# Gated mix of two spectral filters: third row block in two transfers, an eviction moved behind it, two evictions of stage 4 on VectorE, row sums one group sooner

## The chip, the core and the metric

The kernel runs on one core of a Trainium2 chip. That core has five engines that are used here: TensorE (PE; its weight loads are listed apart as PEld), VectorE (DVE), ScalarE (ACT), GpSimd (POOL) and SyncE (SP, which issues most of the DMAs). Each engine works through its own list of instructions in order, and the lists wait for each other through semaphores. The metric is the device time of one execution in microseconds (us); lower is better. The time before is the median of three runs.

## The reference

The input x has 2048 rows of 1024 numbers in bf16. Two branches, A and B, each take a two-dimensional real Fourier transform of x, multiply it with a complex weight of 2048 x 513, and transform back. A gate per row, the sigmoid of the row's product with a vector, mixes the two.

```python
g = sigmoid((x * gate_w).sum(-1, keepdims=True))
def branch(x, w_r, w_i):
    X = rfft2(x.astype(float32)) * (w_r + 1j * w_i)
    return irfft2(X, s=(2048, 1024)).astype(bfloat16)
out = g * branch(x, A_w_r, A_w_i) + (1 - g) * branch(x, B_w_r, B_w_i)
```

## The kernel before

All transforms are matrix products with constant matrices. A list of operations is written down in program order with what each reads and writes (`P.add`); from it each engine gets its own instructions in that same order, with a semaphore wait wherever another engine's result is needed. So the order in the Python text is the order on every engine: an instruction whose wait is not over holds up everything behind it on its engine. A weight or x tile is waited for by the whole transfer that carries it.

The work goes through these stages.

- **Stage 1** (`fold`, `stage1`). The rows come in four blocks, c = 0 to 3, each of 1 MB on 128 partitions; `XPARTS` says in how many transfers, and blocks 2 and 3 lie where weights are loaded later. VectorE folds a block (L348: sums for h = 0, differences for h = 1, each with s = 0, 1). TensorE then makes 32 matmuls a block (L387), in four units (h, j) of eight; each unit fills two of the eight PSUM banks, and is copied to `FT` by ScalarE (L398) or, for three units of blocks 1 to 3, by VectorE (L396). A unit's banks come free for the next block when that copy is done.
- **Weights** (`wload`). 44 transfers on SP's queue, in six lots with a semaphore each. The lots follow x and the constants on the same queue. Lot 2 holds what products 2 to 4 need, lot 3 products 5 and 6, lot 4 product 7, lot 5 (the last) product 8.
- **Stages 2 and 4** (`step(i)`, i = 0 to 15). In each step TensorE does stage 4 of i (L482, two PSUM banks; bank 3 is shared by neighbouring steps, so the second half of stage 4 of i+1 waits for the copy of i), then stage 2 of i+2 (L456, L465), then a few small matmuls for the gate (L514). ScalarE copies both results (L486 for stage 4 into one of six `X` slots, L471 for stage 2). `swap(i)` exchanges real and imaginary rows of the copy by two DMAs, on POOL's queue for i up to 8 and on SP's behind the weights after that.
- **Products** (`product`, L501, VectorE): `ORDER[i]` lists which products come behind step i; the second number of an entry is 0 for the copy itself and 1 for the swapped one. They write the weights' own tiles.
- **Stage 5** (`group`): 32 groups of 16 matmuls (L610) and one copy each (L621 on ScalarE, L619 on VectorE), over four PSUM slots in turn. The first group follows step 14; groups 1 to 7 need the first-half products, of which (8, 0) and (8, 1) with h0 = 0 are the last. The row sums for the gate are finished on VectorE (`row_sums`), spread by 32 matmuls (`zsum`, L557), go through a sigmoid on ScalarE (L560), and become masks (`gate_mask`, L566, VectorE). `rbgen` (L597, VectorE, 16 of them) multiplies the masks into the matrices of stage 6.
- **Stages 6 and 7** for 16 row groups r (L751 copied by L766; L781 with an even part copied by L788). For most r, VectorE makes two sums of PSUM and copy (L828) and POOL adds and subtracts these (L833, 22 in all); for r = 5, 9, 12, 14, 15 VectorE does it alone (L814, L792). Each r ends in a store of 256 KB. Row group 13 is the last that POOL works on.

After the first stage 6 pieces the remaining `rbgen` follow: some at once, then one behind each of the next r. The lines at the end of stage 5 that set the order before are:

```python
group(spare(), g, "dve" if n in (2, 3) else "act")
if n == 2: zsum([spare(), spare()])
if n in (3, 5): gate_mask(n // 2 - 1)
for _ in range((3 < n < 14) + (n == 6)): rbgen(rb.pop(0), "dve")
```

Of the kernel before, what the change touches and what calls it, by code (L numbers as in the profile page):

```python
# [5 lines left out]
ACT = mybir.ActivationFunctionType  # L6
# [228 lines left out]
def bass_gated_mix__spectral_gfnet__spectral_gfnet__prompt_kernel(nc, A_x, A_w_r, A_w_i, B_x, B_w_r, B_w_i, gate_w, out):  # L235
# [36 lines left out]
    def bank(b):  # L272
        return ("ps", b)
# [9 lines left out]
    P = Prog()  # L283
# [12 lines left out]
    def xloc(c):  # L296
        return WT[c // 2], ((c % 2) * 32 + 24) * RWS[c // 2]

    XPARTS = {0: ((0, 1), (1, 1), (2, 2)), 1: ((0, 2), (2, 2)), 2: ((0, 4),), 3: ((0, 2), (2, 2))}
    XALL = [("x", c, q0) for c in range(4) for q0, n in XPARTS[c]]  # L300
    P.add("pool", lambda e: e.memset(sl(CL, GRo, [(1, 256)]), 0.0), w=["GRz"])
    P.add("pool", lambda e: e.memset(DUM[:], 0.0), w=["DUM"])
    for _ in range(18):
        P.add("pe", lambda e: e.matmul(ps(7 * 512, [(1, 256)]), sl(CL, GRo, [(1, 128)]), sl(CL, GRo, [(1, 256)]), start=True, stop=True),
              r=["GRz"], w=[bank(7)])
# [34 lines left out]
    def fold(c, q0, n, h):  # L340
        t, o = xloc(c)
        o += q0 * 1024
        fo = (c % 2) * 4096 + q0 * 1024
        for s in range(2):
            g = 1 - 2 * s
            i0 = sl(t, o + 511 * s, [(1024, n), (256 * g, 2), (g, 128)])
            i1 = sl(t, o + (512 if s else 1023), [(1024, n), (-256 * g, 2), (-g, 128)])
            P.add("dve", lambda e, s=s, i0=i0, i1=i1: e.tensor_tensor(  # L348
                out=sl(XF, fo + h * 512 + s * 256, [(1024, n), (384 - 512 * s, 2), (1, 128)]), in0=i0, in1=i1, op=ALU.subtract if h else ALU.add),
                r=[("x", c, max(a for a, _ in XPARTS[c] if a <= q0))], w=[("xf", c % 2, q, h, s) for q in range(q0, q0 + n)])  # L350

    def folds(c):
        parts = XPARTS[c]
# [17 lines left out]
    def stage1(c):  # L371
        nonlocal cnt
        us = [(cnt + k) % 4 for k in range(4)]
        cnt += 4
        parts = XPARTS[c] if c == 0 else ((0, 4),)
        for q0, n in parts:
            for h in range(2):
                for j in range(2):
                    u = us[2 * h + j]
                    for q in range(q0, q0 + n):  # L380
                        r = 4 * c + q
                        base = (c % 2) * 4096 + q * 1024 + h * 512
                        o = ps(u * 1024 + q * 256, [(1, 256)])
                        for s in range(2):
                            lh = sl(XF, base + 256 * s + 128 * j, [(1, 128)])
                            rh = sl(MM, r * 128, [(2048 * s, 2), (1, 128)])
                            P.add("pe", lambda e, o=o, lh=lh, rh=rh, s=s: e.matmul(o, lh, rh, start=(s == 0), stop=(s == 1)),  # L387
                                  r=[("xf", c % 2, q, h, s ^ j), ("M", c), ("NM", c)], w=[bank(2 * u + q // 2)])
                    if q0 + n < 4:
                        continue  # L390
                    for m0, mn in ((0, 32), (32, 96)) if (c, h, j) == (3, 1, 1) else ((0, 128),):
                        src = ps(u * 1024 + m0, [(128, 2), (1, mn), (256, 4)])
                        dst = sl(FT, h * 8192 + j * 2048 + 16 * m0 + 4 * c, [(4096, 2), (16, mn), (1, 4)])
                        kw = dict(r=[bank(2 * u), bank(2 * u + 1)], a=[("F1", h, j)] + [("F1a", h, j)] * (m0 == 0))
                        if (c, h, j) in ((1, 0, 1), (2, 1, 1), (3, 0, 1)):
                            P.add("dve", lambda e, s=src, d=dst: e.tensor_copy(d, s), **kw)  # L396
                        else:
                            P.add("act", lambda e, s=src, d=dst: e.activation(d, s, ACT.Copy), **kw)  # L398
# [21 lines left out]
    last1 = [P.ops["pe"][-1]]  # L420
    SEQ = [(0, 0), (0, 1), (0, 2), (1, 0)] + [(0, p) for p in range(3, 8)] + [(1, p) for p in range(1, 8)]
    CSo = lambda i: (i % 3) * 1024
    Xk = lambda i: (i + 1) % NX
# [50 lines left out]
    def stage4(i):  # L474
# [8 lines left out]
                                                                                      start=(m == 0), stop=(m == 1)),  # L483
                          r=[("CS", i % 3), "CK"], w=[bank(bk[pm])])
        dst, src = sl(XF, Xo(i), [(1, 1024)]), ps(bk[0] * 512, [(256, 2), (512, 2), (1, 256)])
        P.add("act", lambda e: e.activation(dst, src, ACT.Copy), r=[bank(k) for k in bk], w=[("X", Xk(i))], after=last1)  # L486

    def swap(i):
        eng = ("pool", "sp")[i > 8]
# [133 lines left out]
    def group(u, g, eng):  # L623
        group_mm(u, g, range(8), lambda q: q)
        group_out(u, g, eng, 0, 8, 1, 0, [("Z", 0), ("Z", 1)])
# [27 lines left out]
    def step(i):  # L653
# [5 lines left out]
        if i == 15:  # L659
            dma("sp", "U5", sl(FT, U5o, [(2048, 8), (1, 1024)]).bitcast(u16), cst["U5"].ap().rearrange("p (a b) -> p a b", a=8), w=["U5"], after=[last2])  # L660


    ORDER = (((0, 0),), ((1, 0),), ((2, 0),), ((3, 0),), ((0, 1), (4, 0)), ((1, 1), (2, 1)), ((3, 1),), ((5, 0, 0, 2, 2), (4, 1), (5, 1, 0, 2, 2)),
             ((7, 0), (7, 1)), ((8, 0, 0, 1), (8, 1, 0, 1), (8, 0, 1, 1)), ((8, 1, 1, 1), (9, 0, 0, 2, 2)), ((9, 1, 0, 2, 2),), ((11, 0, 0, 2, 2),),
             ((11, 1, 0, 2, 2),))

    def products(i):
# [22 lines left out]
    def spare():  # L690
        slots.append(slots.pop(0))
        return slots[-1]
# [27 lines left out]
    for n, g in enumerate(range(16, 32)):  # L720
        if n == 14:
            last_groups([spare(), spare()])
        elif n < 14:
            group(spare(), g, "dve" if n in (2, 3) else "act")
        if n == 2:
            zsum([spare(), spare()])
        if n in (3, 5):
            gate_mask(n // 2 - 1)
        for _ in range((3 < n < 14) + (n == 6)):
            rbgen(rb.pop(0), "dve")  # L730
    assert slots[-2:] == [1, 2]
    last5 = P.ops["pe"][-1]

# [114 lines left out]
    stage6_mm(1, range(2, 4), (0,))  # L848
    stage6_mm(1, range(4), (1,))
    stage6(1, False)  # L850
    for _ in range(2):
        rbgen(rb.pop(0), "dve")
    for r in range(16):
        for q in {0: (), 1: (2,), 2: (3, 4)}.get(r, (r + 2,) if r < 14 else ()):
# [69 lines left out]
```

## Time and profile before

| what | value |
|---|---|
| median of three runs | 123.36 us (123.10 to 123.36) |
| the profiled execution's own time | 123.46 us |
| its span, first to last instruction | 121.4 us |
| busy: PE, DVE, ACT, POOL | 114.2, 101.0, 99.5, 40.9 us |
| DMA | 26.11 MB, mean 215 GB/s |
| granted TensorE clock | 1.00 throughout |
| stage 1 on PE | 5.5 to 21.5 us |
| stages 2 and 4 on PE | 21.5 to 50.7 us |
| stage 5 on PE | 50.7 to 84.7 us |
| stages 6 and 7, to the last store | 84.7 to 121.4 us |

Times inside the span are counted from its first instruction. The profiled execution took 2.06 us more than its span; what lies around the span is the same for both kernels as far as the profile tells. The span is read stage by stage, since no single engine is the limit of all four.

### The profile page before, as it was taken

The numbers are of one execution on the slowest core, as the hardware profiler recorded it, in microseconds if no ns is written. First come the engines' busy times: TensorE is split into PE (matmuls) and PEld (weight loads), VectorE is DVE, ScalarE is ACT, GpSimd is POOL, SyncE is SP. The second block draws the span as 40 slices with busy tenths as digits, with TensorE's granted clock in tenths as the row PEclk, the third lists the DMA queues.
The fourth block names the chain that finished last, engine by engine and source line by source line (L and its number), as shares of the span: only waits on it lengthen the run. The fifth ranks groups of instructions, "written<-read, shape, count | busy, mean of one in ns | idle before, by whom it ended". The sixth has DMA issues, their size and how long they took to land.

```text
span 121.4 us, 3690 instructions
## 1 busy us (share of the span) xinstructions
PE 114.2 (94%) x1556; PEld 95.3 (78%) x1556; DVE 101.0 (83%) x160; ACT 99.5 (82%) x119; POOL 40.9 (34%) x47
## 2 busy tenths in 40 slices
PE   6898999999999999999999999999999999999950
PEld 4566688887766766689999999999899969898630
DVE  0378999989798699999999848998689997787890
ACT  4249985999999999999999988999779858867610
POOL 1000042016655600000000000000039999999990
PEclk9999999999999999999999999999999999999999
DMA  3999999999999999840699400000001222424556
GB/s 89 298 406 432 403 326 359 354 348 352 363 361 368 363 363 373 301 173 23 174 397 388 174 0 5 0 5 0 0 5 56 100 102 93 173 86 150 204 200 231
DMA packets 17536, 26.11 MB, mean 215 GB/s; under 512 B 2096, under 2 KB 11056, under 8 KB 17392
## 3 DMA queue, kind: packets, MB, share of 16 engines
q1 hardware_dynamic: 16224, 23.00, 54.0%
q0 software_dynamic: 864, 2.36, 5.4%
q10 hardware_dynamic: 432, 0.52, 1.4%
q8 instruction: 12, 0.20, 0.7%
q14 instruction: 4, 0.03, 0.1%
HBM read 17.48 MB, written 4.19 MB: 178 GB/s over the span
## 4 chain that ended last, share of the span: by engine, by line
PE 71%; POOL 9%; DMA 6%; DVE 3%; issue 3%; SPq 2%; ACT 2%; POOLq 1%; DVEq 0%
PE PS L610 26%; PE PS L482 12%; POOL WA L833 9%; PE PS L751 7%; PE PS L387 7%; PE PS L781 6%; PE PS L456 6%; DMA WB<-in_A_x_dram 6%; PE PS L465 3%; PE PS L514 2%; DVE XF L348 2%; SPq L290 2%; POOLq L863 1%; ACT XF L486 1%; PE PS L557 1%
## 5 line engine op out<-in xcount | busy, mean ns | idle before, releaser
L833 POOL TENSOR_TENSOR WA<-WA 128x512 bf16<-128x512 f32 x22 | 28.5, 1326 | 47.6 <-DVE WA L828 47.6
L610 PE MATMUL PS<-CL,WB 128*128 128x128 bf16 x256 | 31.7, 226 | 0.0
L610 PE MATMUL PS<-CL,WA 128*128 128x128 bf16 x256 | 31.6, 223 | 0.0
L610 PEld LDWEIGHTS PS<-CL,WB 128*128 128x128 bf16 x256 | 31.3, 145 | 0.2
L610 PEld LDWEIGHTS PS<-CL,WA 128*128 128x128 bf16 x256 | 31.3, 145 | 0.1
L621 ACT ACTIVATE WB<-PS 128x1024 bf16<-128x1024 f32 (+1 forms) x30 | 28.4, 1020 | 0.6 <-PE PS L610 0.5
L501 DVE TENSOR_TENSOR WB<-XF,WA 128x2048 bf16<-128x2048 bf16 (+2 forms) x14 | 19.3, 1384 | 2.7 <-ACT XF L486 1.6
L766 ACT ACTIVATE WA<-PS 128x1024 bf16<-128x1024 f32 (+1 forms) x16 | 15.9, 997 | 6.6 <-PE PS L751 6.6
L781 PE MATMUL PS<-FT,WA 128*128 128x256 bf16 (+1 forms) x132 | 19.4, 292 | 0.3 <-DVE WA L828 0.2
L501 DVE TENSOR_TENSOR WA<-MM,WA 128x2048 bf16<-128x2048 bf16 (+2 forms) x14 | 19.2, 1385 | 0.5 <-DMA MM<-XF 0.5
L486 ACT ACTIVATE XF<-PS 128x1024 bf16<-128x1024 f32 x16 | 17.5, 1092 | 0.6 <-DVE WB L501 0.3
L482 PE MATMUL PS<-XF,CK 128*128 128x512 bf16 (+1 forms) x72 | 17.5, 356 | 0.2 <-ACT XF L486 0.2
L471 ACT ACTIVATE XF<-PS 128x1024 bf16<-128x1024 f32 x16 | 17.4, 1093 | 0.1
L387 PE MATMUL PS<-MM,XF 128*128 128x256 bf16 x128 | 15.4, 273 | 1.1 <-DVE XF L348 0.9
L828 DVE TENSOR_TENSOR WA<-PS,WA 128x512 f32<-128x512 f32 x22 | 14.0, 682 | 2.6 <-PE PS L751 1.7
L387 PEld LDWEIGHTS PS<-MM,XF 128*128 128x128 bf16 x128 | 12.0, 98 | 4.7 <-DVE XF L348 3.1
L781 PEld LDWEIGHTS PS<-FT,WA 128*128 128x128 bf16 x132 | 12.2, 98 | 3.8 <-DVE WA L828 0.5
L290 POOL DMA_DIRECT2D MM<-XF x18 | 9.9, 550 | 13.5 <-PE PS L482 7.8
L398 ACT ACTIVATE FT<-PS 128x1024 bf16<-128x1024 f32 (+2 forms) x14 | 12.5, 966 | 2.2 <-PE PS L387 2.2
L348 DVE TENSOR_TENSOR XF<-WB 128x512 bf16<-128x512 bf16 (+1 forms) x20 | 6.0, 366 | 6.1 <-DMA WB<-in_A_x_dram 6.1
L456 PEld LDWEIGHTS PS<-F,FT 128*128 128x128 bf16 x128 | 8.4, 98 | 3.1 <-ACT FT L398 0.2
L456 PE MATMUL PS<-F,FT 128*128 128x128 bf16 x128 | 10.2, 219 | 0.0
(76 smaller groups left out, 137.4 us busy)
## 6 DMA issues: line engine op xcount, KB each, us to landing
out_dram<-WA SPq DMA_DIRECT2D x14, 256.0 KB, 2.1
MM<-XF POOLq DMA_DIRECT2D x18, 128.0 KB, 5.3
FT<-c_U SPq DMA_DIRECT2D x1, 2048.0 KB, 8.9
MM<-XF SPq DMA_DIRECT2D x14, 128.0 KB, 2.9
WB<-in_A_x_dram SPq DMA_DIRECT2D x3, 512.0 KB, 6.1
WA<-in_A_w_r_dram SPq DMA_DIRECT2D x4, 256.5 KB, 6.1
WA<-in_A_w_i_dram SPq DMA_DIRECT2D x4, 256.5 KB, 6.1
WA<-in_B_w_r_dram SPq DMA_DIRECT2D x4, 256.5 KB, 6.2
```

The source lines that it names most:

```text
L387: P.add("pe", lambda e, o=o, lh=lh, rh=rh, s=s: e.matmul(o, lh, rh, start=(s == 0), stop=(s == 1)), r=[("xf", c % 2, q, h, s ^ j), ("M", c ...
L456: P.add("pe", lambda e, o=o, cs=cs, j=j, t=t, rh=rh: e.matmul(o, fblock(1 + cs, j, t), rh, start=(j == 0), stop=(j == 1)), r=[("F1a" if p ...
L471: P.add("act", lambda e: e.activation(dst, src, ACT.Copy), **kw)
L482: P.add("pe", lambda e, o=o, kind=kind, pm=pm, m=m, rh=rh: e.matmul(o, sl(CK, fbo(kind, pm, m), [(1, 128)]), rh, start=(m == 0), stop=(m = ...
L486: P.add("act", lambda e: e.activation(dst, src, ACT.Copy), r=[bank(k) for k in bk], w=[("X", Xk(i))], after=last1)
L501: P.add("dve", lambda e: e.tensor_tensor(out=at(sw), in0=sl(xt, xo + 64 * h0, [(0, 2), (128, 8 * ni), (1, 64 * n)]), in1=at(1), op=ALU.mul ...
L610: P.add("pe", lambda e, o=o, l0=l0, ab=ab: e.matmul(o, sl(WT[ab], l0, [(RWS[ab] // 2, 128)]), sl(CL, KIo[ab], [(1, 128)]), start=(ab == 0) ...
L621: P.add("act", lambda e: e.activation(dst, src, ACT.Copy), r=b, a=keys)
L766: P.add("act", lambda e, s=src, d=dst: e.activation(d, s, ACT.Copy), **kw)
L781: P.add("pe", lambda e: e.matmul(ps(col, [(1, n * 256)]), lh, rh, start=(k == 0), stop=(k == last)), r=[("Y", r), "DI"] + ["DJ"] * (full o ...
L828: P.add("dve", lambda e, s=s, op=op: e.tensor_tensor(out=sl(WA, pq + s * 1024, [(1, 1024)]).bitcast(f32), in0=ps(b0 * 512, [(1, 512)]), in ...
L833: P.add("pool", lambda e, s=s, op=op: e.tensor_tensor(out=ods(s, 0, 2), in0=pv[:, :, 0, :], in1=pv[:, :, 1, :], op=op), r=[("PQ", pk, 0), ...
```

## The change

- Block 2 of x is loaded in two transfers of 512 KB in place of one of 1 MB. A fold now waits for each transfer whose rows it reads.
- Unit (1, 0, 1) of stage 1 is copied by ScalarE in place of VectorE, so VectorE's list goes from the negated constant straight to the folds of block 2.
- The copies of stage 4 for steps 3 and 7 are made by VectorE in place of ScalarE. Some products move to later steps, so that they stand behind these copies: (2, 0) from step 2 to 3, (2, 1) and (3, 1) from steps 5 and 6 to 7, and product 5 with (4, 1) from step 7 to 8.
- At the end of stage 5, VectorE copies group n = 1 alone (before: n = 2 and 3), the row sums' matmuls and sigmoids follow n = 1 (before: n = 2), and both masks and 12 `rbgen` are listed right behind them (before: 11, one or two behind each later group).
- Behind the first pieces of stage 6 come three `rbgen` in place of two, and one behind r = 0 in place of one each behind r = 0, 1 and 2.

```diff
-    XPARTS = {0: ((0, 1), (1, 1), (2, 2)), 1: ((0, 2), (2, 2)), 2: ((0, 4),), 3: ((0, 2), (2, 2))}
+    XPARTS = {0: ((0, 1), (1, 1), (2, 2)), 1: ((0, 2), (2, 2)), 2: ((0, 2), (2, 2)), 3: ((0, 2), (2, 2))}
...
-                r=[("x", c, max(a for a, _ in XPARTS[c] if a <= q0))], w=[("xf", c % 2, q, h, s) for q in range(q0, q0 + n)])
+                r=[("x", c, a) for a, m in XPARTS[c] if a < q0 + n and q0 < a + m], w=[("xf", c % 2, q, h, s) for q in range(q0, q0 + n)])
...
-                        if (c, h, j) in ((1, 0, 1), (2, 1, 1), (3, 0, 1)):
+                        if (c, h, j) in ((2, 1, 1), (3, 0, 1)):
                             P.add("dve", lambda e, s=src, d=dst: e.tensor_copy(d, s), **kw)
...
-        P.add("act", lambda e: e.activation(dst, src, ACT.Copy), r=[bank(k) for k in bk], w=[("X", Xk(i))], after=last1)
+        kw = dict(r=[bank(k) for k in bk], w=[("X", Xk(i))], after=last1)
+        if i in (3, 7):
+            P.add("dve", lambda e: e.tensor_copy(dst, src), **kw)
+        else:
+            P.add("act", lambda e: e.activation(dst, src, ACT.Copy), **kw)
...
-    ORDER = (((0, 0),), ((1, 0),), ((2, 0),), ((3, 0),), ((0, 1), (4, 0)), ((1, 1), (2, 1)), ((3, 1),), ((5, 0, 0, 2, 2), (4, 1), (5, 1, 0, 2, 2)),
-             ((7, 0), (7, 1)), ((8, 0, 0, 1), (8, 1, 0, 1), (8, 0, 1, 1)), ((8, 1, 1, 1), (9, 0, 0, 2, 2)), ((9, 1, 0, 2, 2),), ((11, 0, 0, 2, 2),),
+    ORDER = (((0, 0),), ((1, 0),), (), ((2, 0), (3, 0)), ((0, 1), (4, 0)), ((1, 1),), (), ((2, 1), (3, 1)),
+             ((5, 0, 0, 2, 2), (4, 1), (5, 1, 0, 2, 2), (7, 0), (7, 1)), ((8, 0, 0, 1), (8, 1, 0, 1), (8, 0, 1, 1)), ((8, 1, 1, 1), (9, 0, 0, 2, 2)), ((9, 1, 0, 2, 2),), ((11, 0, 0, 2, 2),),
              ((11, 1, 0, 2, 2),))
...
-            group(spare(), g, "dve" if n in (2, 3) else "act")
-        if n == 2:
+            group(spare(), g, "dve" if n == 1 else "act")
+        if n == 1:
             zsum([spare(), spare()])
-        if n in (3, 5):
-            gate_mask(n // 2 - 1)
-        for _ in range((3 < n < 14) + (n == 6)):
-            rbgen(rb.pop(0), "dve")
+            gate_mask(0)
+            gate_mask(1)
+            for _ in range(12):
+                rbgen(rb.pop(0), "dve")
...
-    for _ in range(2):
+    for _ in range(3):
         rbgen(rb.pop(0), "dve")
```

## The prediction

> **What bounds the kernel now.** I read the sums by stage first, then the waits inside each stage, then the chain of work that ended last, then timelines where the chain leaves PE. A stage's gain counts only up to what ends the next wait, so I looked at each hand-over. The waits between 24 and 50.7 us (us in total, times, longest):
>
> ```profile
> PEld PS L482 <- ACT XF L486: 5.2, 13, 0.7
> DVE WB L501 <- ACT XF L486: 1.6, 2, 1.1
> DVE WB L501 <- DMA WA<-in_B_w_i_dram: 1.1, 2, 0.8
> ```
>
> In stages 2 and 4 ScalarE is never idle (26.5 of 26.7 us): two copies a step, one every 0.915 us, make the step 1.83 us. While ScalarE kept up, a step took PE 1.745 us. From PE's start-to-start times, the halves of L482 that wait for the shared bank lose 0.05 + 0.07 + 9 x 0.08 + 0.37 = 1.22 us. The third line is weights not yet there. Now the hand-over to stage 5, chain and VectorE timeline:
>
> ```profile
> 49.07 1.15 ACT XF L486
> 50.21 0.05 issue
> 50.26 0.60 PE PS L482 x2
> 50.87 0.96 PE PS L610 x16
> ```
> ```profile
> 47.68 1.23 DVE L501 TENSOR_TENSOR WA<-MM,WA 128x2048 bf16<-128x2048 bf16 x1
> 49.18 0.70 DVE L501 TENSOR_TENSOR WB<-XF,WA 128x1024 bf16<-128x1024 bf16 x1 [0.27 <-DMA WA<-in_B_w_i_dram]
> 49.80 0.70 DVE L501 TENSOR_TENSOR WA<-MM,WA 128x1024 bf16<-128x1024 bf16 x1
> ```
>
> The chain blames ScalarE, but the second product of step 8, which group 1 needs, ends at 50.50, and L610's first matmul starts at 50.70. Its release is 0.20 us from being the bound. Ahead of it stands a DMA: lot 5 of the weights lands at 49.08, VectorE starts 0.10 later. Behind 50.7 PE runs stage 5 without a hole. In the tail:
>
> ```profile
> 96.83 0.45 PE PS L781 x4
> 97.28 0.04 DVEq L224
> 97.32 0.15 DVE WA L828
> 97.47 0.05 issue
> 97.52 1.04 PE PS L781 x4
> ...
> 117.14 1.22 POOL WA L833
> ```
> ```profile
> L833 POOL TENSOR_TENSOR WA<-WA 128x512 bf16<-128x512 f32 x22 | 28.5, 1326 | 47.6 <-DVE WA L828 47.6
> ```
> ```profile
> 86.63 1.28 DVE L597 TENSOR_TENSOR XF<-FT,MM 128x1024 bf16<-128x1024 bf16 x2
> 88.53 1.29 DVE L828 TENSOR_TENSOR WA<-PS,WA 128x512 f32<-128x512 f32 x2 [0.62 <-ACT WA L788]
> 89.74 0.68 DVE L597 TENSOR_TENSOR MM<-FT,MM 128x1024 bf16<-128x1024 bf16 x1
> 90.52 1.29 DVE L828 TENSOR_TENSOR WA<-PS,WA 128x512 f32<-128x512 f32 x2
> 91.73 1.61 DVE L597 TENSOR_TENSOR MM<-FT,MM 128x1024 bf16<-128x1024 bf16 x1
> ```
>
> POOL works from 89.91 to 118.36 without a gap and its last result makes the last store. The three L597 in this stretch last 0.68, 1.61 and 1.79 us (0.69 alone), and POOL's starts beside them are 1.61, 1.70 and 1.69 us apart (1.235 elsewhere). They also delay row group 3's sums to 97.46, for which PE stands: 0.52 us between two starts that are 0.11 apart elsewhere, 0.41 lost.
>
> **The change, part by part.**
>
> *Stage 1.* The 1 MB transfer lands at 13.18, the next two of 512 KB 1.27 and 1.28 later, so the first half should land near 11.9. Taking the copy (1, 0, 1) out of VectorE's list saves its 1.14 us from start to next start. Folds of the first half then start at 12.40 instead of 13.54, those of the second at about 13.20, the last of the 14 ends its slot at 17.76 instead of 18.76. PE, which stood from 13.83 to 15.02 with five short bursts between, can run its 64 matmuls of blocks 2 and 3 at 0.109 each from 13.83 to 20.81, against 21.47: 0.65 earlier. ScalarE takes one more copy (0.92): its last of block 1 ends at 15.9, PE needs that bank at 16.45, so it is hidden by 0.5. If it were not, stage 1 would lose at most 0.4 of the 0.65. SP issues one DMA more: 0.57 twice for 0.68 once, 0.5 us later for all that follows on SP's queue: F2, gate vector, CK, masks, all weights, CL, the swaps from step 9 on. Issue to landing is 5.2 us or more for every weight transfer and DMA is busy 90% or more until 45 us, so this costs nothing while that backlog lasts; without it up to 0.57 at lot 5.
>
> *Stages 2 and 4.* Each moved copy takes 1.22 us on VectorE (three rows of L396: the same shape from PSUM) and frees 0.915 of ScalarE. With VectorE idle at that time, PE's next half step wants the bank about 1.15 us after the copy starts, so each costs PE some 0.16. ScalarE gets a lead of 1.8 us, and most of the 1.22 goes. PE would reach group 1 near 50.69 - 0.65 - 1.22 + 0.32 = 49.1.
>
> VectorE's list: copy 3 at 29.95 to 31.1; lot 2 of the weights (landing 31.11, product at 31.20 before) still starts (2, 0) at 31.20; (3, 0), (0, 1), (4, 0), (1, 1) follow to 36.94; copy 7 at 37.1; (2, 1) and (3, 1) to 40.57. Before, VectorE idled there (0.47 and 1.09). Product 5 started at 40.95: the profile names L486, but that copy had ended at 37.3; lot 3 landed at 40.86. So product 5 stays at 40.95, and (4, 1), (5, 1), both 7 and step 8's two follow as before. Nothing of it lies ahead of lot 5. Swaps 8 to 10 now queue behind (2, 1), (3, 1) and (4, 1), which read the slots they overwrite; those end at 39.4, 40.6 and 44.3, each before POOL or SP would issue.
>
> So of 1.5 us won on PE, what reaches stage 5 is from 50.70 to 50.50 + 0.05: **0.15 us**. Bounds: nothing less than -0.6 (lot 5 later by the extra issue's 0.57 and VectorE pushed a little), nothing over 1.5 (if lot 5 were not the gate). I take 0.15, as the rows of landing and start lie 0.10 apart.
>
> What weakens it is lot 3, since the swaps on POOL's queue now come up to 0.85 earlier, 0.46 of a pair of 256 KB. At the 365 GB/s of these slices that is 0.32 us of transfer ahead of lot 3. After product 5 the list has 0.35 to spare before lot 5, so 0.32 is covered; if it were 0.85, the gate would be 0.5 later. The Trainium skill, page DMA: Bandwidth & Descriptors, section Queues, rings and completion order, has each DMA engine take turns between the queues at packet granularity. By that rule half of the 0.85 is taken from the weights, 0.43 in place of 0.32, and the sum would be 0.08 worse; no row here shows single engines.
>
> *End of stage 5.* Row sums are ready on VectorE at 69.58 and PE would come for them near 70.0 (71.15 less one group of 0.975, less 0.15): 0.4 to spare. ScalarE has the two sigmoids (1.01 each) and two copies (0.915) in 3.86 us of PE; it runs 0.6 behind and wins back 0.07 a group until group 26. Four PSUM slots give PE over 1 us of cover, so this costs 0; without it 0.6. Masks start at 72.6, four of 0.5, then 12 L597 of 0.60: done near 82, before VectorE's next copy at 83.2. Hidden by the idle VectorE.
>
> *Tail.* Three L597 behind L764 instead of two: the third takes 0.60 of the 0.62 in which VectorE waited for L788 before 88.53. It costs 0 to 0.1. Two L597 leave the stretch with POOL. Without them row group 2's sums come at L788's pace, row group 3's end at 96.2 instead of 97.46, and PE's 0.41 goes (bounds 0.2 to 0.41: no row of the tail shows what waits next, but other row groups of PE show no hole). POOL itself wins 2 x 0.46 = 0.92. The last pair of row group 13 is ready at 115.67 and POOL takes it at 115.88; with VectorE 0.15 + 0.41 earlier, ready at 115.11, and POOL free at 114.85, it starts 0.085 after being ready, 115.19, and ends 0.15 + 0.41 + 0.125 = **0.69** earlier. The o15 stores come 0.56 earlier and land before it.
>
> The Trainium skill, page SBUF — State Buffer, section Terms, calls the port pair of VectorE and GpSimd an exclusive lock held for a whole instruction, the loser fully blocked. By that, POOL would win 2 x 0.69 rather than 0.92, and still be held by row group 13's sums: that sum stays 0.69, against 0.92 + 0.15 if POOL were alone the end.
>
> The sum: span 121.4 - 0.69 = 120.7, time 123.46 - 0.69 = 122.77 against the profiled execution. The median of three lies 0.10 below that execution, so the prediction against it is **122.7 us**.
>
> **Rivals.**
>
> *The weights aren't the gate.* If lot 5 lands earlier because something ahead of it moves, PE's 1.5 us pass on: 123.36 - 1.5 - 0.54 = 121.3. For it: the chain names ScalarE. Against it: VectorE starts 0.10 after a landing, and DMA has no holes to fill.
>
> *Weights later.* Lot 5 later by 0.57, the extra issue: 0.69 - 0.57 = 0.12 gain, 123.25; lot 3 later by 0.85, 0.18 gain, 123.2. For it: SP issues back to back from 0.7 to 52 us. Against: the backlog.
>
> *The tail does not move.* VectorE's sums wait for PE and ScalarE anyway, or the triple L597 delays POOL's start, which then holds the end: 123.36 - 0.15 = 123.2.
>
> *The clock falls (slower).* The change makes a hole of some 1.4 us on PE before 50.5, and none so long is in the trace after 5.5 us. If the granted clock were halved there, as in the 18 opening matmuls (0.213 apart against 0.109 for the same shape later), some 3.6 us at half speed would cost about 1.8: 122.7 + 1.8 = 124.5. It decides as soon as the clock needs 0.7 us of work to come back. The Trainium skill, page TensorE: Matmul & The Clock Gate, Part 1, gives an idle window of about 3.4 us before the clock halves; by that rule this rival has no chance, and no run here shows the limit.
>
> **How the numbers follow.** Forecast 0.55, own range 122.35 to 123.0 (gate 0.3 either way). Weights not the gate 0.08. Weights later 0.11. Tail unmoved 0.14. Clock or another wait that makes it slower 0.12. Within 0.2% (0.25 us: about what this kernel's measurement can tell, its three runs span 0.26) lie 123.11 to 123.61. Faster: 0.55 + 0.08 = 0.63. Same: 0.11 + 0.14 = 0.25. Slower: 0.12. The range takes in forecast, later weights and unmoved tail, 122.3 to 123.5, and leaves out 0.20.
>
> **What would show it.** Right: PE stands over 1 us before L610's first matmul, and VectorE starts step 8's product 0.1 after a weight landing near 49.1; stage 1 ends near 20.8; L482 waits on VectorE at two steps; one long L597 beside POOL; no wait of L781 for L828 near 97; POOL's last operation 0.7 earlier. Wrong: L610 starts before 50 or after 51; PE waits for L557's input; POOL's last pair is ready as late as before; PEclk under 1.

## The result, and the profile after

The changed kernel takes 122.16 us (median of 4 runs, 122.01 to 122.39) against 123.36 on the same chip: a ratio of 0.9907 with a 95% interval of 0.9885 to 0.9930, so a gain of 1.15 us with 0.86 to 1.42. The forecast was 122.7, a gain of 0.66. The sign was right; the gain is 1.7 times as large, and the time lies below the low end of the range, 122.3.

The profiled execution took 122.14 us with a span of 120.1, against 123.46 and 121.4 before. To the hundredth the two spans are 121.43 and 120.09, 1.34 apart, and that difference can be laid out along marks that both traces have. In the changed kernel's line numbers, L387 is unchanged and L482 too, L486 has become L490 (L488 where VectorE makes the copy), L501 is L505, L597 is L601, L610 is L614, and everything behind is 4 higher.

| mark (us from the span's start) | before | after | gain up to here |
|---|---|---|---|
| second half of x block 1 has landed | 10.03 | 9.78 | 0.25 |
| stage 1's last matmul starts | 21.36 | 20.45 | 0.91 |
| second half of stage 4 of step 14 starts | 50.26 | 49.31 | 0.95 |
| stage 5's second matmul starts (it needs step 8's second product) | 50.76 | 50.03 | 0.73 |
| POOL's last operation ends | 118.36 | 117.16 | 1.20 |
| span ends | 121.43 | 120.09 | 1.34 |

So 0.73 comes from the front, 0.47 from between stage 5's start and POOL's end, 0.14 from behind it. The prediction had 0.15, 0.54 and nothing for these.

First the hand-over to stage 5. The waits of the changed kernel between 24 and 50.7 us (us in total, times, longest):

```profile
PEld PS L482 <- ACT XF L490: 4.1, 11, 0.7
ACT XF L471 <- PE PS L465: 1.0, 2, 0.5
PEld PS L482 <- DVE XF L488: 1.0, 2, 0.5
DVE WB L505 <- DMA WA<-in_B_w_i_dram: 0.4, 2, 0.3
```

Two new lines stand here. PE now waits for VectorE's two copies (the third line), and ScalarE, which had almost no idle time in this stretch, stands 1.0 us for PE (the second): the work that it was relieved of turned into idle time, not into a lead. The chain that ended last, over the same stretch (start, us, what):

```profile
30.23 10.42 DMA WA<-in_B_w_i_dram
...
40.74 1.61 DVE WB L505
...
48.66 0.70 DVE WB L505
49.36 0.63 DVE WA L505
49.98 0.05 issue
50.03 1.13 PE PS L614 x15
```

Before, the chain came to stage 5 over ScalarE and PE. Now it comes over VectorE's products, which start at 40.74, right behind the landing of lot 3 of the weights at 40.65. The timelines of VectorE and of PE:

```profile
47.48 1.23 DVE L505 TENSOR_TENSOR WA<-MM,WA 128x2048 bf16<-128x2048 bf16 x1
48.66 0.70 DVE L505 TENSOR_TENSOR WB<-XF,WA 128x1024 bf16<-128x1024 bf16 x1
49.27 0.70 DVE L505 TENSOR_TENSOR WA<-MM,WA 128x1024 bf16<-128x1024 bf16 x1
```
```profile
49.31 0.61 PE L482 MATMUL PS<-XF,CK 128*128 128x512 bf16 x2 [0.21 <-ACT XF L490]
49.76 0.22 PE L614 MATMUL PS<-CL,WB 128*128 128x128 bf16 x1
50.03 0.27 PE L614 MATMUL PS<-CL,WA 128*128 128x128 bf16 x1
```

Step 8's first product starts at 48.66, 0.10 behind the landing of lot 5 (48.56), as before; but before that landing came at 49.08. Its second product ends at 49.97, and L614's second matmul, the first to read it, starts at 50.03, 0.27 behind the first where 0.06 is the spacing. PE's own arrival, VectorE's list and the landing now meet within 0.3 us: with the product there, L614's second matmul would have followed its first at 49.82, and VectorE's list, 1.14 us from product to product, would have come to step 8 at 48.62 without the landing.

The tail, in the changed kernel's group of POOL's sums, VectorE's timeline and the chain:

```profile
L837 POOL TENSOR_TENSOR WA<-WA 128x512 bf16<-128x512 f32 x22 | 27.6, 1290 | 48.2 <-DVE WA L832 48.2
```
```profile
86.56 1.29 DVE L601 TENSOR_TENSOR MM<-FT,MM 128x1024 bf16<-128x1024 bf16 x2
87.86 1.29 DVE L832 TENSOR_TENSOR WA<-PS,WA 128x512 f32<-128x512 f32 x2
89.07 0.68 DVE L601 TENSOR_TENSOR MM<-FT,MM 128x1024 bf16<-128x1024 bf16 x1
89.86 1.29 DVE L832 TENSOR_TENSOR WA<-PS,WA 128x512 f32<-128x512 f32 x2
92.54 1.29 DVE L832 TENSOR_TENSOR WA<-PS,WA 128x512 f32<-128x512 f32 x2 [1.39 <-ACT WA L792]
```
```profile
95.27 0.89 PE PS L755 x16
96.17 1.30 PE PS L785 x8
97.47 0.89 PE PS L755 x16
```

One L601 is left beside POOL and it takes 0.68; behind the next two sums VectorE is idle 1.39 us. PE's stage 7 of row group 3 is one unbroken piece of 1.30 us, where it was 0.45, a wait on L828, and 1.04. POOL's operations take 1290 ns on average in place of 1326; its first two starts are 1.61 us apart, as before, and the next ones 1.23 to 1.24, where two more gaps were 1.70 and 1.69. And POOL, which worked without a gap to its end, now waits before its last pair:

```profile
111.82 2.49 POOL L837 TENSOR_TENSOR WA<-WA 128x512 bf16<-128x512 f32 x2
114.66 2.50 POOL L837 TENSOR_TENSOR WA<-WA 128x512 bf16<-128x512 f32 x2 [0.34 <-DVE WA L832]
```

### The profile page after: what moved, and what is told of

Same layout as the page of the kernel before. It is cut to its first block, busy times and chain, and to the rows that moved or that the text cites. A ratio compares the mean times of both kernels' runs of the same rounds, so it can differ in the third digit from the quotient of the medians.

```text
span 120.1 us, 3690 instructions
## 1 busy us (share of the span) xinstructions
PE 114.1 (95%) x1556; PEld 95.9 (80%) x1556; DVE 99.5 (83%) x160; ACT 99.0 (82%) x119; POOL 38.4 (32%) x47
## 4 chain that ended last, share of the span: by engine, by line
PE 59%; SPq 18%; DMA 9%; DVE 8%; issue 3%; ACT 1%; POOL 0%; DVEq 0%; POOLq 0%
PE PS L614 26%; SPq L290 18%; PE PS L785 14%; PE PS L755 11%; DMA WA<-in_B_w_i_dram 9%; DVE WA L505 3%; PE PS L304 3%; DVE WB L505 3%; PE PS L387 2%; DVE WA L796 1%; PE PS L561 1%; PE PS L482 1%; PE PS L588 1%; ACT WB L625 1%; DVEq L867 0%
## 5 line engine op out<-in xcount | busy, mean ns | idle before, releaser
L837 POOL TENSOR_TENSOR WA<-WA 128x512 bf16<-128x512 f32 x22 | 27.6, 1290 | 48.2 <-DVE WA L832 48.2
L614 PE MATMUL PS<-CL,WB 128*128 128x128 bf16 x256 | 31.8, 226 | 0.0
L614 PE MATMUL PS<-CL,WA 128*128 128x128 bf16 x256 | 31.7, 223 | 0.1
L614 PEld LDWEIGHTS PS<-CL,WB 128*128 128x128 bf16 x256 | 31.3, 145 | 0.3 <-DVE WB L505 0.2
L614 PEld LDWEIGHTS PS<-CL,WA 128*128 128x128 bf16 x256 | 31.3, 145 | 0.3 <-DVE WA L505 0.2
L505 DVE TENSOR_TENSOR WB<-XF,WA 128x2048 bf16<-128x2048 bf16 (+2 forms) x14 | 19.3, 1384 | 1.0 <-ACT XF L490 0.5
L505 DVE TENSOR_TENSOR WA<-MM,WA 128x2048 bf16<-128x2048 bf16 (+2 forms) x14 | 19.2, 1385 | 0.0
L482 PE MATMUL PS<-XF,CK 128*128 128x512 bf16 (+1 forms) x72 | 17.5, 356 | 0.2 <-ACT XF L490 0.2
L471 ACT ACTIVATE XF<-PS 128x1024 bf16<-128x1024 f32 x16 | 16.7, 1052 | 1.1 <-PE PS L465 1.0
L490 ACT ACTIVATE XF<-PS 128x1024 bf16<-128x1024 f32 x14 | 14.7, 1050 | 1.4 <-PE PS L482 0.6
L387 PE MATMUL PS<-MM,XF 128*128 128x256 bf16 x128 | 15.4, 280 | 0.3 <-DVE XF L348 0.3
L387 PEld LDWEIGHTS PS<-MM,XF 128*128 128x128 bf16 x128 | 12.5, 100 | 3.3 <-DVE XF L348 1.4
L398 ACT ACTIVATE FT<-PS 128x1024 bf16<-128x1024 f32 (+2 forms) x15 | 13.1, 1012 | 0.9 <-PE PS L387 0.9
```

Source lines behind the costliest of these rows:

```text
L471: P.add("act", lambda e: e.activation(dst, src, ACT.Copy), **kw)
L482: P.add("pe", lambda e, o=o, kind=kind, pm=pm, m=m, rh=rh: e.matmul(o, sl(CK, fbo(kind, pm, m), [(1, 128)]), rh, start=(m == 0), stop=(m = ...
L490: P.add("act", lambda e: e.activation(dst, src, ACT.Copy), **kw)
L505: P.add("dve", lambda e: e.tensor_tensor(out=at(sw), in0=sl(xt, xo + 64 * h0, [(0, 2), (128, 8 * ni), (1, 64 * n)]), in1=at(1), op=ALU.mul ...
L614: P.add("pe", lambda e, o=o, l0=l0, ab=ab: e.matmul(o, sl(WT[ab], l0, [(RWS[ab] // 2, 128)]), sl(CL, KIo[ab], [(1, 128)]), start=(ab == 0) ...
L837: P.add("pool", lambda e, s=s, op=op: e.tensor_tensor(out=ods(s, 0, 2), in0=pv[:, :, 0, :], in1=pv[:, :, 1, :], op=op), r=[("PQ", pk, 0), ...
```

## The experiments

Theories, by the letters that the expectations use:

- A: front and tail each bring their part and the parts add up. Stage 5 begins when both PE and step 8's second product are there, and that product follows the landings of lots 3 and 5. The two copies of stage 4 bring nothing, because ScalarE stands idle for what it is relieved of.
- B: the front brings 0.15, as forecast, and what is missing comes from the tail.
- C: ScalarE's relief in stage 4 opens the way into stage 5.
- D: the change itself makes lot 5 land sooner.
- E: the two edits of stage 1 need each other.
- F: the tail's gain comes from two L597 fewer beside POOL.
- G: the tail's gain needs the earlier row sums.

All medians and ratios are against the kernel before on the same chip, and edits are relative to the kernel before unless the text says otherwise. Four hunks of the change's diff are named below: *split* (`XPARTS` and the fold's reads), *copy* (unit (1, 0, 1)), *stage 4* (copies 3 and 7, `ORDER`), *tail* (row sums, masks and `rbgen`).

**Front alone.** Split, copy and stage 4; the tail as before.

```diff
-    XPARTS = {..., 2: ((0, 4),), ...}
+    XPARTS = {..., 2: ((0, 2), (2, 2)), ...}
-                        if (c, h, j) in ((1, 0, 1), (2, 1, 1), (3, 0, 1)):
+                        if (c, h, j) in ((2, 1, 1), (3, 0, 1)):
...
+        if i in (3, 7):
+            P.add("dve", lambda e: e.tensor_copy(dst, src), **kw)
```

> All edits up to stage 5 (block 2 in two transfers, copy (1,0,1) on ScalarE, stage 4's copies 3 and 7 on VectorE with the new product order); the end of stage 5 and the tail are those of before. Theory A (front and tail add up, the front worth the 0.67 us by which stage 5 began earlier in the changed kernel, the tail 0.54): 122.7 us, 0.67 under before. Theory B (the front is worth 0.15 as predicted and the rest came from the tail): 123.2.

Measured: 122.96 (122.48 to 124.09) against 123.44; ratio 0.9981 [0.9958, 1.0003]. By the medians a gain of 0.48, by the ratio 0.23 with -0.04 to 0.52: single times of this kernel scatter over 1.6 us, those of the kernel before over 0.5. In the profile (122.91) stage 5's second matmul starts at 50.20, 0.56 sooner than before, and the span, 120.88, is 0.55 shorter. The profile is against B's 0.15; the interval of the times holds both.

**Tail alone.**

```diff
-            group(spare(), g, "dve" if n in (2, 3) else "act")
-        if n == 2:
+            group(spare(), g, "dve" if n == 1 else "act")
+        if n == 1:
             zsum([spare(), spare()])
-        if n in (3, 5):
-            gate_mask(n // 2 - 1)
-        for _ in range((3 < n < 14) + (n == 6)):
-            rbgen(rb.pop(0), "dve")
+            gate_mask(0)
+            gate_mask(1)
+            for _ in range(12):
+                rbgen(rb.pop(0), "dve")
...
-    for _ in range(2):
+    for _ in range(3):
         rbgen(rb.pop(0), "dve")
```

> Only the end of stage 5 and the tail (row sums one group sooner, 12 + 3 + 1 L597 instead of 11 + 2 + 3). Theory A: PE's 0.41 hole near 97 goes and POOL takes row group 13 sooner by 0.125, 122.8 us, 0.54 under before, stage 5 still begins near 50.7. Theory B: 1.0 under before, 122.3.

Measured: 122.74 (122.39 to 123.16); ratio 0.9946 [0.9928, 0.9964], a gain of 0.67 [0.44, 0.89]. Its stage 5 starts where it did before (50.74), and from there POOL's end comes in 67.01 us against 67.60. With the front's 0.48 by medians, 0.55 by the profiled spans, and this kernel's 0.70 and 0.74, the two parts make 1.18 or 1.29, where the whole change makes 1.20 or 1.34; by the ratios it is 0.90 of 1.15, with intervals that hold the difference. The parts add up, as A has it, and the tail holds more of the gain than the front, but not all that was missing, as B would have it.

**Stage 1 alone.** Split and copy.

> Only block 2 in two transfers and copy (1,0,1) on ScalarE. PE should reach group 1 some 0.65 to 0.9 us sooner than 50.70. Theory A (PE and step 8's product are both near the gate, and the product moves with the landing of the weights): 0.2 to 0.7 under before, 122.7 to 123.2, the larger if lot 5 lands near 48.6, the smaller if near 49.1. Theory C (the saving of ScalarE in stage 4 is what opened the gate): at most 0.15 under before, 123.2.

Measured: 123.20 (122.83 to 124.26); ratio 0.9982 [0.9965, 1.0000]. In the profile (122.83) stage 1's last matmul starts at 20.38 and stage 5's second at 50.10. By the times, a gain of 0.22 with 0.00 to 0.43, this run can't part A from C; by the marks stage 5 starts 0.66 sooner with stage 4 untouched, which falls to A.

**Stage 4 alone.**

```diff
+        if i in (3, 7):
+            P.add("dve", lambda e: e.tensor_copy(dst, src), **kw)
+        else:
+            P.add("act", lambda e: e.activation(dst, src, ACT.Copy), **kw)
...
-    ORDER = (((0, 0),), ((1, 0),), ((2, 0),), ((3, 0),), ((0, 1), (4, 0)), ((1, 1), (2, 1)), ((3, 1),), ...
+    ORDER = (((0, 0),), ((1, 0),), (), ((2, 0), (3, 0)), ((0, 1), (4, 0)), ((1, 1),), (), ((2, 1), (3, 1)), ...
```

> Only stage 4's copies 3 and 7 on VectorE with the new product order. Theory A: ScalarE stands idle for what it was relieved of, since it can't copy what PE has not made; L482's waits still add up to some 1.2 us: within 0.1 of before, 123.3. Theory C: 0.5 under before or more, 122.8.

Measured: 123.36 (123.15 to 123.63) against 123.44; ratio 0.9999 [0.9988, 1.0009]: nothing. The waits between 24 and 50.7 us of this kernel, and the first copy that ScalarE makes behind the one that it no longer makes:

```profile
PEld PS L482 <- ACT XF L490: 4.1, 11, 0.7
ACT XF L471 <- PE PS L465: 1.0, 2, 0.5
PEld PS L482 <- DVE XF L488: 1.0, 2, 0.5
ACT XF L490 <- PE PS L482: 0.6, 3, 0.2
```
```profile
31.29 1.02 ACT L471 ACTIVATE XF<-PS 128x1024 bf16<-128x1024 f32 x1 [0.51 <-PE PS L465]
```

They are the lines of the changed kernel. At each moved copy ScalarE waits 0.51 us for stage 2's matmuls and 0.18 for the next stage 4, 0.69 of the 0.915 that it was relieved of. From the first L482 to the second half of step 14's stage 4 it takes 26.16 us, against 26.19 in every kernel whose copies are on ScalarE. That falls to A and against C. It isn't free on VectorE either: in this run product 5 starts at 41.31, 1.32 behind lot 3 (39.99), and step 8's first product at 49.18, 0.48 behind lot 5 (48.70), so here VectorE's list and not the weights sets when the products are done. PE came later still, at 50.58.

**The changed kernel once more**, for the spread of its marks from execution to execution.

> The changed kernel once more. Theory A (stage 5 of the changed kernel begins when PE and step 8's product are both there, the latter following the landing of weight lots 3 and 5): median 122.2, single runs scattered wider than before's 0.5 us, since the landings scatter; lot 5 lands between 48.5 and 49.1. Theory D (the profiled run of before had a typical landing of 49.08 and the change itself makes lot 5 land 0.5 sooner): lot 5 lands at 48.6 or less here.

Measured: 122.25 (121.99 to 122.42) against 123.41; ratio 0.9898 [0.9882, 0.9914]. Its lot 5 landed at 48.70, 0.14 later than in the first profile and not at 48.6 or less as D had it, and stage 5's second matmul started at 50.16.

**The changed kernel without stage 4.** Copies 3 and 7 and `ORDER` as before.

> The changed kernel without its stage 4 part: copies 3 and 7 back on ScalarE and the product order of before. Theory A (that part brings nothing, since ScalarE stands idle for what it is relieved of): within 0.1 of the changed kernel, 122.2. Theory C (it opens the gate together with stage 1's gain): 0.25 slower than the changed kernel, 122.45 or more.

Measured: 122.40 (122.17 to 123.00); ratio 0.9921 [0.9899, 0.9944]. The median is 0.15 above the changed kernel's, between A's 0.1 and C's 0.25, and 0.28 by the ratios, but the two intervals overlap, this kernel's single times scatter over 0.83 us, and the spans of the profiles are 120.10 here, 120.09 and 120.23 there. No part of the 1.15 us is shown to need stage 4's edit; that it brings a little beside the other edits is not ruled out.

**Less weight, in the changed kernel.** To take away the landing as a cause, branch B's part of lot 2 isn't loaded (1.05 MB, twice what the expectation says; POOL sets those rows to zero instead). Lots 3 to 5 stand behind it on the same queue and land sooner.

```diff
+    P.add("pool", lambda e: e.memset(sl(WA, 40 * RW, [(1, 8 * RW)]), 0.0), w=[("W", 2)])
...
-            for f in range(2):
+            for f in range(1 if key == 2 else 2):
```

> The changed kernel with branch B's half of weight lot 2 left out of the loads (0.5 MB; those weights are zeros written by POOL at the start), so that lots 3 to 5 land some 1.4 us sooner. Theory A: step 8's product is no longer late, PE goes straight on from 49.76: 0.2 to 0.3 faster than the changed kernel, 121.9, with less scatter. Theory B (weights don't gate): no difference, 122.2.

Measured: 122.25 (122.13 to 122.39); ratio 0.9899 [0.9882, 0.9916], the same as with all weights, where A had expected 121.9. Lots 3 and 5 landed at 35.72 and 45.10, 4.9 and 3.5 us sooner than in the first profile of the changed kernel, yet step 8's products ran from 48.77 to 50.07, since VectorE's own list came to them only then. PE arrived at 50.17, in an execution whose x came late (10.19 against 9.78). So in the changed kernel the landing is one of three limits that lie together; taking it away uncovers the other two.

**Less weight, in the kernel before.** The same edit.

> The kernel before with the same half lot left out. Theory A: PE comes to stage 5 at 50.7 by itself and the weights are there sooner in most runs: within 0.1 of before, 123.4. If lot 5 were the gate of before in most runs: 0.2 faster or more.

Measured: 123.47 (123.23 to 123.74) against 123.41; ratio 1.0003 [0.9991, 1.0014]: nothing. VectorE's and PE's timelines of this kernel (its lines behind L302 are one higher):

```profile
48.05 0.69 DVE L502 TENSOR_TENSOR WB<-XF,WA 128x1024 bf16<-128x1024 bf16 x1
48.66 0.70 DVE L502 TENSOR_TENSOR WA<-MM,WA 128x1024 bf16<-128x1024 bf16 x1
```
```profile
50.45 0.60 PE L483 MATMUL PS<-XF,CK 128*128 128x512 bf16 x2 [0.21 <-ACT XF L487]
50.89 0.22 PE L611 MATMUL PS<-CL,WB 128*128 128x128 bf16 x1
```

The product that group 1 needs is done at 49.36, 1.5 us before PE comes. So PE is what bounded the kernel before here, and weights that land 3.8 us sooner (45.24) are worth nothing to it.

**Split alone.**

```diff
-    XPARTS = {..., 2: ((0, 4),), ...}
+    XPARTS = {..., 2: ((0, 2), (2, 2)), ...}
-                r=[("x", c, max(a for a, _ in XPARTS[c] if a <= q0))], ...
+                r=[("x", c, a) for a, m in XPARTS[c] if a < q0 + n and q0 < a + m], ...
```

> Only block 2 in two transfers; copy (1,0,1) stays on VectorE in front of block 2's folds. Theory E (the two edits of stage 1 need each other: VectorE reaches the folds at 13.54, when the whole block has been there since 13.2): stage 1 still ends at 21.3, within 0.1 of before, 123.4. If the split alone carried the gain: stage 1 ends at 20.7, 122.9.

Measured: 123.28 (123.02 to 123.51) against 123.31; ratio 0.9998 [0.9987, 1.0008]: nothing. VectorE still makes the copy (L396) when the first half has landed, and the folds start behind it:

```profile
11.79 1.22 DVE L396 CAST FT<-PS 128x1024 bf16<-128x1024 f32 x1
12.92 3.29 DVE L348 TENSOR_TENSOR XF<-WA 128x512 bf16<-128x512 bf16 x8
```

The same run shows the gate that the prediction described. Its x and with it PE were early, but its lot 5 landed at 49.28, the latest of all:

```profile
49.38 0.70 DVE L501 TENSOR_TENSOR WB<-XF,WA 128x1024 bf16<-128x1024 bf16 x1
50.00 0.69 DVE L501 TENSOR_TENSOR WA<-MM,WA 128x1024 bf16<-128x1024 bf16 x1
```
```profile
49.64 0.60 PE L482 MATMUL PS<-XF,CK 128*128 128x512 bf16 x2 [0.21 <-ACT XF L486]
50.39 0.25 PE L610 MATMUL PS<-CL,WB 128*128 128x128 bf16 x1
50.75 0.27 PE L610 MATMUL PS<-CL,WA 128*128 128x128 bf16 x1
```

PE stands until 50.39 and again until 50.75. With the usual 0.44 from that half of stage 4 it would have begun at 50.08. The second wait is for step 8's second product, which ends at 50.69. The first is not for a product, though the profile names one: step 8's first product had ended at 50.08. PE's list waits there for the constant `CL`, which L610 also reads and which SP loads right behind the weights; it landed at 50.25. The same landing comes at 50.06 in the kernel before and at 49.54 in the changed one, 0.98 behind lot 5 in both.

**Copy alone.**

```diff
-                        if (c, h, j) in ((1, 0, 1), (2, 1, 1), (3, 0, 1)):
+                        if (c, h, j) in ((2, 1, 1), (3, 0, 1)):
```

> Only copy (1,0,1) on ScalarE; block 2 in one transfer, landing near 13.1. The folds can start at 13.2 instead of 13.5. Theory E: stage 1 ends 0.3 sooner, 21.0, and stage 5 begins 0.3 sooner, 123.1. If the folds were not what PE waits for: no change.

Measured: 123.00 (122.72 to 124.03) against 123.31; ratio 0.9979 [0.9962, 0.9996], a gain of 0.26 [0.05, 0.47]. The folds of block 2 now wait for the whole megabyte:

```profile
13.05 3.30 DVE L348 TENSOR_TENSOR XF<-WA 128x512 bf16<-128x512 bf16 x8 [0.72 <-DMA WA<-in_A_x_dram]
```

So E is half right: the copy is worth something alone and the split isn't. In stage 1's own time the two together are worth twice the copy (0.66 against 0.33, next sections); the times of the whole kernel, 0.22 with 0.00 to 0.43 for both, don't show that.

**One `rbgen` more, sooner, without moving the row sums.** 12, 3 and 1 as in the change, with groups, row sums and masks as before.

```diff
-        for _ in range((3 < n < 14) + (n == 6)):
+        for _ in range((3 < n < 14) + (n in (6, 8))):
...
-    for _ in range(2):
+    for _ in range(3):
         rbgen(rb.pop(0), "dve")
```

> Row sums where they were; only one L597 more in the late groups of stage 5 (12 in place of 11), three behind the first stage 6 pieces, one behind r = 0. Theory F (the tail's gain is two L597 fewer beside POOL and in front of row group 3's sums): PE's hole near 97 goes, 0.6 to 0.7 under before, 122.8; VectorE's copies of group 30 come 0.4 later but ScalarE's are later still. Theory G (the earlier row sums are needed): the twelfth L597 delays group 30's copy and stage 6 by 0.4, 123.2.

Measured: 122.85 (122.67 to 122.95) against 123.31; ratio 0.9960 [0.9947, 0.9974], a gain of 0.49 [0.32, 0.65]. In its chain PE's hole near 97 is gone:

```profile
95.83 0.89 PE PS L751 x16
96.72 1.30 PE PS L781 x8
98.02 0.89 PE PS L751 x16
```

**Row sums sooner, with as many `rbgen` beside POOL as before.** 11, 2 and 3.

```diff
-            group(spare(), g, "dve" if n in (2, 3) else "act")
-        if n == 2:
+            group(spare(), g, "dve" if n == 1 else "act")
+        if n == 1:
             zsum([spare(), spare()])
-        if n in (3, 5):
-            gate_mask(n // 2 - 1)
-        for _ in range((3 < n < 14) + (n == 6)):
-            rbgen(rb.pop(0), "dve")
+            gate_mask(0)
+            gate_mask(1)
+            for _ in range(11):
+                rbgen(rb.pop(0), "dve")
```

> Row sums, masks and 11 L597 one group sooner, but two L597 behind the first stage 6 pieces and three beside POOL as before. Theory F: within 0.1 of before, 123.4, PE's hole near 97 as before. Theory G: 0.3 or more under before.

Measured: 123.34 (123.02 to 123.59) against 123.31; ratio 0.9997 [0.9985, 1.0009]: nothing. VectorE's long L597 are back:

```profile
91.64 1.60 DVE L597 TENSOR_TENSOR MM<-FT,MM 128x1024 bf16<-128x1024 bf16 x1
...
94.36 1.79 DVE L597 TENSOR_TENSOR MM<-FT,MM 128x1024 bf16<-128x1024 bf16 x1
```

These two runs settle F against G: the tail's gain comes with two L597 fewer beside POOL, and the earlier row sums bring nothing by themselves.

**All profiles side by side** (us from the span's start; "x" is the landing of block 1's second half, "stage 1" its last matmul's start, "stage 4" the time from the first L482 to the second half of step 14's, "product" the end of step 8's second product, "stage 5" the start of its second matmul, "to POOL" from there to POOL's last end, "store" from there to the span's end):

| kernel | x | stage 1 less x | stage 4 | lot 5 | product | stage 5 | to POOL | store |
|---|---|---|---|---|---|---|---|---|
| before | 10.03 | 11.33 | 26.19 | 49.08 | 50.49 | 50.76 | 67.60 | 3.07 |
| split alone | 9.41 | 11.33 | 26.19 | 49.28 | 50.69 | 50.75 | 67.67 | 3.04 |
| copy alone | 9.88 | 11.00 | 26.19 | 48.38 | 49.79 | 50.28 | 67.64 | 3.04 |
| stage 1 alone | 9.71 | 10.67 | 26.19 | 48.63 | 50.04 | 50.10 | 67.63 | 3.06 |
| stage 4 alone | 9.95 | 11.33 | 26.16 | 48.70 | 50.48 | 50.64 | 67.59 | 3.08 |
| front alone | 10.08 | 10.68 | 26.16 | 48.74 | 50.15 | 50.20 | 67.64 | 3.04 |
| row sums alone | 9.63 | 11.33 | 26.20 | 49.15 | 50.55 | 50.61 | 67.61 | 3.07 |
| `rbgen` alone | 9.91 | 11.33 | 26.19 | 48.75 | 50.15 | 50.64 | 67.07 | 2.92 |
| tail alone | 10.01 | 11.33 | 26.19 | 48.53 | 49.94 | 50.74 | 67.01 | 2.94 |
| changed, no stage 4 | 10.09 | 10.67 | 26.19 | 48.60 | 50.01 | 50.16 | 67.02 | 2.92 |
| changed | 9.78 | 10.67 | 26.15 | 48.56 | 49.97 | 50.03 | 67.13 | 2.93 |
| changed, again | 9.93 | 10.68 | 26.16 | 48.70 | 50.10 | 50.16 | 67.12 | 2.95 |

The two kernels with less weight, not in the table, fit its first columns (10.67 and 11.33). Read down a column, "stage 1 less x" takes three values to within 0.01, and which it is depends on the two edits of stage 1 alone; "to POOL" and "store" take two, which depend on how many L597 stand beside POOL. "Lot 5" goes with no edit: over the twelve executions it lies from 48.38 to 49.28, with 48.65 as the mean of the five with both edits of stage 1 and 48.77 as that of the six without any split (before, stage 4, copy, row sums, `rbgen`, tail). That difference of 0.1 under a spread of 0.9 doesn't bear out D. Four of the kernels (before, row sums, `rbgen`, tail) are the same up to that landing, and it came between 48.53 and 49.15 in them, so most of the spread is between executions and not between edits.

## Why the prediction was right, and where it was not

**Stage 1 was right.** Forecast 0.65, measured 11.33 - 10.67 = 0.66. The steps were right too: the folds of block 2 start when the negated constant is done. The "changed" timeline of VectorE:

```profile
11.82 0.42 DVE L365 TENSOR_SCALAR MM<-MM 128x1024 bf16<-128x1024 bf16 x1
12.15 4.21 DVE L348 TENSOR_TENSOR XF<-WA 128x512 bf16<-128x512 bf16 x10
```

They start at 12.15, where the forecast was 12.40 for an x that came 0.25 later, and the first half of block 2 had landed at 11.74 (forecast 11.9). Alone the copy gives 0.33, since the folds then wait for the whole landing, and the split gives 0, since VectorE is still copying. The remaining 0.25 of the 0.91 in the first table is an earlier landing of block 1 in that execution; it has nothing to do with the edits, as the "x" column shows (9.41 to 10.09).

**Stage 4 was wrong, without an effect on the sum.** "ScalarE gets a lead of 1.8 us, and most of the 1.22 goes. PE would reach group 1 near 50.69 - 0.65 - 1.22 + 0.32 = 49.1" is a step that failed, though not the one that made the sum too small. The cost to PE was right: some 0.16 a copy forecast, 0.17 measured at the half of L482 that waits for it. The saving was not, since ScalarE can't copy what PE has not yet made. It stood 0.69 us a moved copy, so only 0.23 of 0.915 was a lead. By PE's start-to-start times each moved copy turns three losses of 0.08 into 0.17, 0 and 0.05, and then they are back at 0.08; L482's losses went from 1.22 to 1.19 in all. PE reached group 1 at 49.76, not near 49.1; and `CL`, whose landing at 49.54 the sum left out, would not have let it start much before 49.7. The run with stage 4 alone shows that the edit brings nothing by itself, and the changed kernel without it shows no loss clear of its scatter.

**The gate is the step that made the forecast fail: 0.15 forecast, 0.73 in the profiled pair.** The step was "what reaches stage 5 is from 50.70 to 50.50 + 0.05". It took the 50.50 of one execution as fixed, because VectorE started 0.10 behind a landing. That landing, 49.08, was the third latest of twelve. At the median of 48.70 the product is done 1.41 later, at 50.11, and stage 5 may start its second matmul near 50.17: 0.59 under the 50.76 before, which is nearly all of stage 1's 0.66. So the mechanism was right (in the split-only run PE did wait at this gate, and the changed kernel's second matmul starts 0.06 behind the product), but its place was read off a late execution; that the profiled one was late was bad luck, and taking it without a spread was the mistake. The run on the kernel before with less weight shows what the one profile couldn't: the landing had no hold on that kernel's time. In the five full-load profiles with both edits of stage 1, stage 5's second matmul starts at 50.03 to 50.20, with a mean of 50.13. That is 0.63 sooner than in the one profile before, and 0.56 sooner than the mean of 50.69 over the six full-load profiles whose stage 1 takes 11.33. By the prediction's own signs this is the part that was wrong: it had PE stand over 1 us before L610 and called a start before 50 a sign of failure; PE stood 0.27 us between L614's first two matmuls, and the first started at 49.76.

By the times the front alone brought less than in its profile (0.48 by medians, 0.23 by the ratio, against 0.55). Single times of the three kernels that have the copy moved and the old tail reach 124.03 to 124.26. None of those executions was profiled, so what they lost stays open; a lot 5 as late as 49.28, with stage 5 at the 50.75 of the split-only run, would account for some 0.6 of the 1.0 to 1.1 that they lie above their medians.

**The tail was right in mechanism and nearly in size.** Forecast 0.54 (0.41 of PE's hole plus 0.125), measured 67.60 less 67.01 to 67.13, so 0.47 to 0.59. PE's hole is gone, and the forecast that POOL's last pair would then wait for row group 13's sums instead of following on is borne out: it waited 0.34 us. The forecast had it ready at 115.11 with the front's 0.15, which is 114.53 with 0.73; it was ready at 114.58. The part of the change that does this is smaller than forecast: one `rbgen` more before the tail and three instead of two at its head, without any move of the row sums. The Trainium skill, page SBUF — State Buffer, section Terms, has VectorE and GpSimd lock each other out of a shared port pair for whole instructions; the trace agrees in that both sides' long times go together (L597 of 1.61 and 1.79 us and POOL's starts 1.70 and 1.69 apart before, 0.68 and 1.23 after). The size that the prediction drew from that rule, 0.69 a piece for POOL, is not what the trace has: POOL lost 0.46 at each of the two.

**A term was missing: 0.13 behind POOL.** From POOL's last end to the span's end it takes 3.04 to 3.08 us in the seven kernels with the old tail and 2.92 to 2.95 in the five with the new one. Before, POOL's result left on SP's queue 0.05 to 0.10 us behind the last store on ScalarE's queue, and landed 2.48 to 2.52 us after its issue. With the tail shorter on POOL's side SP's store goes first and lands in 2.21 to 2.27; ScalarE's, 0.03 to 0.11 behind it, takes 2.32 to 2.41 and is now the last to land (119.61 against 119.44 in the profile after). Of the 0.13, 0.07 lies between POOL's end and the last landing and 0.06 behind that landing. Both go with the order of the two stores, but no run changed that order alone, so the cause isn't shown. The prediction said only that ScalarE's stores "land before it".

**The rivals.** "The weights aren't the gate" came nearest for the front: not since something ahead of lot 5 moved, but since the landing is usually earlier than in the profile that was read. For its 1.5 us to pass on whole, `CL` too would have had to land a good deal sooner than the 50.06 of the trace that was read. "Weights later" did not come: with the extra issue on SP's queue lot 5 landed at a mean of 48.75 over six executions, without it at 48.77 over six. By the estimate that the prediction worked out from the Trainium skill, page DMA: Bandwidth & Descriptors, section Queues, rings and completion order, the gate was to be 0.08 later than the forecast. A shift of that size lies far under the 0.9 between the twelve landings, so no run here can tell. "The tail does not move" is ruled out by the tail-only run. The clock did not fall: PE's hole before stage 5 was 0.27 us, not 1.4, and the granted clock read 1.00 through it. It reads 1.00 over the opening matmuls as well, so the halving that this rival took from their spacing (0.213 against 0.109) is not in any profile's clock row.

## What to carry to other kernels

A DMA landing read from one execution is one draw: before it is made a fixed gate, its spread over executions has to enter the range, and a run with less to load tells cheaply whether it holds anything up. An engine that copies the results of another can't bank the time it is relieved of beyond what the buffers between them hold: count the lead by those buffers, not by the instruction taken away. When two edits clear the same spot (data that lands sooner, an engine that is free sooner), the first alone may show nothing, so try them together before either is dropped.

## What the runs showed of the hardware that was not expected

- The last lot of the 44 weight transfers lands between 48.53 and 49.15 us in four executions whose instructions are the same up to there, and between 48.38 and 49.28 in all twelve with full load. Block 1 of x, near the head of that queue and ahead of every edit, lands between 9.41 and 10.09 in the twelve. What comes between fixed hand-overs is far steadier: stage 1 from x to its end is the same to 0.01 us among kernels with the same stage 1, and so is stage 4 among those with the same copies.
- Lots 3 and 5 came 3.5 to 5.8 us sooner when 1.05 MB ahead of them was left out, which at the 365 GB/s of that stretch is 2.9 us of transfer. Why it is more than that stays open.
- Two stores of the last results on different queues, issued 0.03 to 0.11 us apart, take 2.0 to 2.3 us for the first and 2.3 to 2.5 for the second. The seven kernels in which ScalarE's goes first end 0.13 us later behind POOL than the five in which SP's does; whether the order is the cause is not shown.
